# Putting the words of float64 weights together in two PSUM banks instead of in SBUF

## The chip, the cores and the metric

One core of one Trainium2 chip runs the whole program. The metric is the device time of one execution in microseconds (us); of several executions the median counts. Engines are named as the profile names them: PE (TensorE), DVE (VectorE), ACT (ScalarE), POOL (GpSimd) and SP (SyncE, which here issues the DMAs).

## The reference

Three stages follow each other: local and global attention, a dense layer pair with SiLU, and a soft mixture of experts.

```python
scores = scale * q @ k.T + bias          # 4 x 8 heads, 768 positions, 64 wide, banded
x = softmax(scores) @ v                  # 3072 tokens x 512
h = x @ w_in                             # 512 x 2048
x2 = (h * (1.0 / (1.0 + np.exp(-h)))) @ w_out   # 2048 x 512
logits = x2 @ phi                        # 32 slots
# softmax over tokens gathers x2 into slots, experts w1, w2 work on the slots,
# softmax over slots spreads the result over the tokens again
```

`w_in` and `w_out` arrive as float64, all other large inputs as float32. The kernel has to turn the float64 words into numbers that TensorE can multiply.

## The kernel before, in words

Every float32 number goes through TensorE as two float16 parts, a high one and a low one, and a product takes three matmuls. A part pair is made by the helpers `hi` (lines 191 to 195: one scaled copy on ACT, POOL or DVE) and `lo` (lines 199 and 201: value minus high part, on POOL or DVE).

The 3072 tokens are 24 tiles of 128, worked in 8 chunks of 3 tiles. Attention of a tile is a list of items: `split` (makes the parts of q, k and v), `s_step` (scores into the banks `bS`: matmuls of line 293, then line 298 on DVE and the exponential of line 299 on ACT), and `pv_step` (matmuls of line 336 into `bPV`, scaled by line 346). The first tiles run alone; after that the attention items of the next chunk are dealt out between the matmul steps of the present one. A chunk has 16 steps `l1_step` (lines 460 to 462, then tanh in line 464, line 466 and the parts), and then `l2_part` (lines 480 to 482). The order on each engine is not the order of the Python code: a scheduler with a cost model arranges the instructions at build time.

PSUM has eight banks of 128 x 512 float32: `bS` two, `bPV` one, `bW` four in rotation for the steps of both layers, and `bM` one for small sums.

The weights come in 16 pieces of 1 MB (eight of `w_in`, eight of `w_out`); `w_ahead` has SP load the next one as soon as its place in SBUF is free, and `conv(p)` turns piece p into float16 parts. A piece holds 1024 float64 numbers in each partition. What `conv` does to a piece, by line:

- 421 (DVE) makes a 16-bit check value from each high word, and 423 (PE, twice) sums it over the partitions into `bM`;
- 426 (POOL, pieces 2, 3, 4 and 10) or 428 (ACT, the other twelve) writes the top three bits of the low word's mantissa as a 16-bit number over the low half of the low word, in SBUF;
- 429 (DVE) writes the sign over the upper half, and 430 (DVE) xors the shifted high word in: the low word now is a float32 number;
- 440 (ACT) makes the high part;
- 448 (DVE, 11 pieces) makes the low part, or 443 (ACT) and 446 (POOL) do for pieces 0, 3, 6, 9 and 10.

Piece 0 is turned early in the attention of the first tiles, pieces 1 to 7 between the first layer's steps of chunk 0, and pieces 8 to 15 between the second layer's steps of chunk 0. From chunk 1 on there are no weights left to turn.

Of the kernel before, what the change touches and what calls it, by code (L numbers as in the profile page):

```python
# [45 lines left out]
def p2(e):  # L46
    return float(2.0 ** e)
# [39 lines left out]
L3E = 'AAPPPAAAAAPAAAAA'  # L87
LOE = 'PVVPVVPVVPPVVVVV'
# [12 lines left out]
def fast_kernel(tc, keepp, q_l, k_l, v_l, q_f, k_f, n_global, n_local, w_in, w_out, phi, w1, w2, shapes, pick_c, out):  # L101
# [8 lines left out]
    with ExitStack() as ctx:  # L110
# [8 lines left out]
        bank = [psp.tile([128, 512], F32, name=f"bank{i}") for i in range(8)]  # L119
        bS, bPV, bW, bM = bank[0:2], bank[2], bank[3:7], bank[7]  # L120
        turn = [0]
# [6 lines left out]
        one16 = ar.new([2], BF16)  # L128
# [285 lines left out]
        def conv(p):  # L414
# [6 lines left out]
            V.tensor_scalar(out=odd16.bitcast(U16), in0=u16[:, :, 3], scalar1=0x7000, scalar2=0x3000, op0=ALU.bitwise_and, op1=ALU.bitwise_xor)  # L421
            for j in range(2):
                mm(bM[0:1], one16[:, 0:1], odd16[:, 512 * j:512 * j + 512], start=(p + j == 0), stop=(p + j == 16))

            if L3E[p] == "P":
                G.tensor_scalar(out=u16[:, :, 0], in0=by[:, :, 3], scalar1=1.0 / 32, scalar2=-0.484375, op0=ALU.mult, op1=ALU.add)
            else:
                A.activation(out=u16[:, :, 0], in_=by[:, :, 3], func=AF.Copy, scale=1.0 / 32, bias=-0.484375)
            V.tensor_scalar(out=u16[:, :, 1], in0=u16[:, :, 3], scalar1=0x8000, scalar2=None, op0=ALU.bitwise_and)  # L429
            V.scalar_tensor_tensor(out=low, in0=high, scalar=3, in1=low, op0=ALU.logical_shift_left, op1=ALU.bitwise_xor)  # L430
            lowf = ar.view(place[p], [1024, 2], F32)[:, :, 0]
            if p < 8:
                dst = [wih[:, z, :, 256 * p:256 * p + 256] for z in range(2)]
                src = lowf.rearrange("p (k f) -> p k f", k=4)
# [49 lines left out]
        def l2_end(c, m):  # L484
            op = bW[(turn[0] + m) % 4]
# [219 lines left out]
        odd16 = ar.view(ext0 + 16384, [1024], BF16)  # L705
# [12 lines left out]
        G.memset(one16, 1.0)  # L718
# [38 lines left out]
        for c in range(NCH):  # L757
# [34 lines left out]
            if c == 0:  # L792
# [8 lines left out]
                V.memset(odd, 0.0)  # L801
                V.tensor_reduce(out=odd[0:1], in_=bM[0:1], axis=AX.X, op=ALU.max)
# [30 lines left out]
            if c < NCH - 1:  # L833
                turn[0] += n
# [390 lines left out]
```

## Time and profile before

| what | value |
| --- | --- |
| time, median of 3 runs | 766.43 us (765.55 to 767.75) |
| profiled execution, own time | 765.0 us |
| its span, first to last instruction | 763.2 us |
| mean granted TensorE clock | 0.964 |
| PE busy | 683.0 us, 89% |
| DVE busy | 489.0 us, 64% |
| ACT busy | 336.6 us, 44% |
| POOL busy | 324.7 us, 43% |

The shares are means over stages that have different limits, so they say little by themselves. The profiled execution lies 1.8 us over its span, and 1.4 us under the median.

### The profile page before, as it was taken

The page shows a single profiled execution, that of the slowest core. Times are in us where ns is not written, and L with a number is a line of the kernel's source. Part 1 is how long each engine was busy: PE and PEld are TensorE (multiplying, and loading weights), DVE is VectorE, ACT ScalarE, POOL GpSimd, SP SyncE. Part 2 cuts the span into 40 slices and gives each one's busy share as a digit, 9 for nine tenths or more (in the row PEclk, how much of TensorE's full clock was granted, in tenths as well). Part 3 has the DMA queues.
Part 4 walks back from the last instruction along what each step waited for, and adds up shares of the span by engine and source line. Part 5 has one row for each costly group of instructions (what it writes and reads, how often), then busy time and mean ns, then how long its engine had stood idle before and what let it go on. Part 6 is the DMA issues. An engine that isn't in the chain of part 4 may idle for free.

```text
span 763.2 us, 14337 instructions
## 1 busy us (share of the span) xinstructions
PE 683.0 (89%) x5559; PEld 395.0 (52%) x5559; DVE 489.0 (64%) x1108; ACT 336.6 (44%) x855; POOL 324.7 (43%) x267
## 2 busy tenths in 40 slices
PE   2477757598999999999999999999999999998995
PEld 1244423244655565556556654665466546665375
DVE  6999999997775487548735873597266306505232
ACT  7756786553552255245423542454156305303122
POOL 4689684733455356415633673337324320101000
PEclk9978969799999999999999999999999999999997
DMA  6787645565456355733563567354532694295987
GB/s 237 194 249 205 218 87 152 191 181 120 75 125 139 83 113 137 174 75 77 132 138 74 107 137 167 56 111 109 86 43 43 150 320 178 97 357 214 391 330 223
DMA packets 162747, 120.22 MB, mean 158 GB/s; under 512 B 137456, under 2 KB 147184, under 8 KB 156656
## 3 DMA queue, kind: packets, MB, share of 16 engines
q1 hardware_dynamic: 162672, 119.23, 58.4%
q8 instruction: 45, 0.74, 0.4%
q14 instruction: 30, 0.25, 0.1%
HBM read 79.10 MB, written 6.29 MB: 112 GB/s over the span
## 4 chain that ended last, share of the span: by engine, by line
PE 67%; DVE 16%; issue 5%; POOL 4%; DMA 4%; ACT 3%; SPq 0%; ACTq 0%; DVEq 0%; POOLq 0%
PE bank L480 8%; PE bank L481 8%; PE bank L482 8%; PE bank L460 8%; PE bank L462 8%; PE bank L461 8%; PE bank L293 4%; PE bank L336 3%; DVE arena L201 2%; DMA arena<-arena 2%; DVE arena L199 2%; POOL arena L193 2%; PE bank L864 2%; DVE arena L429 2%; PE bank L902 2%
## 5 line engine op out<-in xcount | busy, mean ns | idle before, releaser
L193 POOL TENSOR_SCALAR arena<-arena 128x1024 f16<-128x1024 f32 (+5 forms) x146 | 144.4, 1002 | 237.0 <-ACT arena L299 102.5
L460 PE MATMUL bank<-rows,arena 128*128 128x384 f16 x512 | 168.4, 330 | 6.2 <-ACT arena L191 4.0
L462 PE MATMUL bank<-rows,arena 128*128 128x384 f16 x512 | 168.3, 329 | 0.8 <-DVE arena L448 0.8
L461 PE MATMUL bank<-rows,arena 128*128 128x384 f16 x512 | 168.3, 329 | 0.0
L191 ACT ACTIVATE arena<-bank 128x384 f16<-128x384 f32 (+2 forms) x165 | 81.8, 505 | 177.0 <-DVE bank L466 98.7
L199 POOL TENSOR_TENSOR arena<-arena 128x1024 f16<-128x1024 f32 (+2 forms) x69 | 131.0, 1900 | 41.3 <-ACT arena L191 37.3
L299 ACT ACTIVATE arena<-arena 128x256 f32<-128x256 f32 (+1 forms) x192 | 92.2, 482 | 98.2 <-DVE arena L298 95.3
L481 PE MATMUL bank<-arena 128*128 128x512 f16 x336 | 128.9, 384 | 2.7 <-POOL arena L446 1.9
L480 PE MATMUL bank<-arena 128*128 128x512 f16 x336 | 129.1, 384 | 1.5 <-DVE arena L201 1.5
L482 PE MATMUL bank<-arena 128*128 128x512 f16 x336 | 128.7, 383 | 0.0
L201 DVE SCALAR_TENSOR_TENSOR arena<-bank,arena 128x384 f16<-128x384 f32 (+2 forms) x142 | 81.3, 572 | 32.7 <-ACT arena L191 32.0
L293 PE MATMUL bank<-arena 128*128 128x256 f16 (+3 forms) x432 | 63.4, 288 | 41.5 <-DVE arena L298 23.9
L298 DVE CUSTOM_DVE_ANT_0 arena<-bank,arena 128x256 f32<-128x256 f32 (+1 forms) x192 | 70.5, 395 | 44.2 <-PE bank L293 42.8
L466 DVE SCALAR_TENSOR_TENSOR bank<-arena,bank 128x384 f32<-128x384 f32 x128 | 71.2, 557 | 31.0 <-ACT arena L464 29.8
L199 DVE TENSOR_TENSOR arena<-arena 128x1024 f16<-128x1024 f32 (+2 forms) x50 | 74.7, 1496 | 12.6 <-POOL arena L193 12.2
L464 ACT ACTIVATE arena<-bank 128x384 f32<-128x384 f32 x128 | 61.9, 484 | 21.1 <-PE bank L462 20.8
L293 PEld LDWEIGHTS <-arena 128*128 128x128 f16 (+1 forms) x432 | 36.3, 101 | 66.5 <-issue 38.1
L462 PEld LDWEIGHTS <-arena 128*128 128x128 f16 x512 | 50.4, 99 | 35.4 <-issue 1.6
L461 PEld LDWEIGHTS <-arena 128*128 128x128 f16 x512 | 50.4, 98 | 34.5 <-issue 7.2
L460 PEld LDWEIGHTS <-arena 128*128 128x128 f16 x512 | 50.5, 99 | 31.4 <-issue 2.9
L482 PEld LDWEIGHTS <-arena 128*128 128x128 f16 x336 | 33.1, 99 | 43.9 <-issue 5.3
L480 PEld LDWEIGHTS <-arena 128*128 128x128 f16 x336 | 33.2, 99 | 38.1 <-issue 4.8
(174 smaller groups left out, 808.8 us busy)
## 6 DMA issues: line engine op xcount, KB each, us to landing
arena<-in_w_dram SPq DMA_DIRECT2D x31, 1024.0 KB, 7.4
arena<-in_q_l_dram SPq DMA_DIRECT2D x18, 512.0 KB, 3.7
arena<-in_k_l_dram SPq DMA_DIRECT2D x18, 512.0 KB, 4.0
arena<-in_w_in_dram SPq DMA_DIRECT2D x8, 1024.0 KB, 5.7
arena<-in_w_out_dram SPq DMA_DIRECT2D x8, 1024.0 KB, 4.9
arena<-in_v_l_dram SPq DMA_DIRECT2D x24, 256.0 KB, 3.0
out_dram<-arena SPq DMA_DIRECT2D x4, 768.0 KB, 7.6
out_dram<-arena SPq DMA_DIRECT2D x8, 384.0 KB, 5.0
```

Source lines behind the costliest of these rows:

```text
L191: A.activation(out=out, in_=in_, func=AF.Copy, scale=p2(e))
L193: G.tensor_scalar(out=out, in0=in_, scalar1=p2(e), scalar2=0.0, op0=ALU.mult, op1=ALU.add)
L199: (V if eng == "V" else G).tensor_tensor(out=out, in0=in_, in1=h, op=ALU.subtract)
L201: V.scalar_tensor_tensor(out=out, in0=in_, scalar=p2(e), in1=h, op0=ALU.mult, op1=ALU.subtract)
L293: mm(sp[i][:, :w] if t == 0 else sp[i].rearrange("p (s c) -> p s c", s=2), qd[r, 4 * y + h], kv, start=(j == 0), stop=(j == len(terms) - 1))
L299: A.activation(out=pw, in_=pw, func=AF.Exp, scale=-1.0, bias=nmx[:, T, h:h + 1], accum_out=psum_[T % 2][:, h:h + 1])
L460: mm(hp, wh, x[:, 0, k], start=(k == 0), stop=False)
L461: mm(hp, wh, x[:, 1, k], start=False, stop=False)
L462: mm(hp, wl, x[:, 0, k], start=False, stop=(k == 3))
L480: mm(op, gh, woh[:, f, 0], start=(f == 0), stop=False)
L481: mm(op, gh, woh[:, f, 1], start=False, stop=False)
L482: mm(op, gl, woh[:, f, 0], start=False, stop=(f == 15))
```

## The change

`bank6` and `bank7` become one tile `words` (`bC`). ACT writes the three bits of all 16 pieces there as 32-bit integers, DVE adds the sign and the high word there, and both parts are read from there: the high one by ACT, the low one by DVE. POOL has no part in `conv` any more. The place of a piece in SBUF is given up as soon as the word is complete. The check is a bitwise or that DVE keeps over all pieces, without matmuls; one mask and one maximum follow at the end. While words are in the two banks, chunk 0 has three banks of `bW` for its steps instead of four.

```diff
-        bank = [psp.tile([128, 512], F32, name=f"bank{i}") for i in range(8)]
+        bank = [psp.tile([128, 512], F32, name=f"bank{i}") for i in range(6)]
+
+        bC = psp.tile([128, 1024], F32, name="words")
+        bank += [bC[:, 0:512], bC[:, 512:1024]]
...
-                tb = bW[flips[0] % 4]
+                tb = bW[flips[0] % 3]
...
-            V.tensor_scalar(out=odd16.bitcast(U16), in0=u16[:, :, 3], scalar1=0x7000, scalar2=0x3000, op0=ALU.bitwise_and, op1=ALU.bitwise_xor)
-            for j in range(2):
-                mm(bM[0:1], one16[:, 0:1], odd16[:, 512 * j:512 * j + 512], start=(p + j == 0), stop=(p + j == 16))
-
-            if L3E[p] == "P":
-                G.tensor_scalar(out=u16[:, :, 0], in0=by[:, :, 3], scalar1=1.0 / 32, scalar2=-0.484375, op0=ALU.mult, op1=ALU.add)
-            else:
-                A.activation(out=u16[:, :, 0], in_=by[:, :, 3], func=AF.Copy, scale=1.0 / 32, bias=-0.484375)
-            V.tensor_scalar(out=u16[:, :, 1], in0=u16[:, :, 3], scalar1=0x8000, scalar2=None, op0=ALU.bitwise_and)
-            V.scalar_tensor_tensor(out=low, in0=high, scalar=3, in1=low, op0=ALU.logical_shift_left, op1=ALU.bitwise_xor)
-            lowf = ar.view(place[p], [1024, 2], F32)[:, :, 0]
+            V.scalar_tensor_tensor(out=odd16, in0=u16[:, :, 3], scalar=0x3000, in1=odd16, op0=ALU.bitwise_xor, op1=ALU.bitwise_or)
+
+            word = bC.bitcast(I32)
+            A.activation(out=word, in_=by[:, :, 3], func=AF.Copy, scale=1.0 / 32, bias=-0.484375)
+            V.scalar_tensor_tensor(out=word, in0=high, scalar=-(2 ** 31), in1=word, op0=ALU.bitwise_and, op1=ALU.bitwise_xor)
+            V.scalar_tensor_tensor(out=word, in0=high, scalar=3, in1=word, op0=ALU.logical_shift_left, op1=ALU.bitwise_xor)
+            holder[place[p]] = None
+            w_ahead()
...
             A.activation(out=dst[0], in_=src, func=AF.Copy, scale=-p2(e - 128))
-            if LOE[p] != "V":
-                if LOE[p] == "P":
-                    A.activation(out=src, in_=src, func=AF.Copy, scale=-p2(e - 128))
-                else:
-                    G.tensor_scalar(out=src, in0=src, scalar1=-p2(e - 128), scalar2=0.0, op0=ALU.mult, op1=ALU.add)
-                G.tensor_tensor(out=dst[1], in0=src, in1=dst[0], op=ALU.subtract)
-            else:
-                V.scalar_tensor_tensor(out=dst[1], in0=src, scalar=-p2(e - 128), in1=dst[0], op0=ALU.mult, op1=ALU.subtract)
-            holder[place[p]] = None
-            w_ahead()
+            V.scalar_tensor_tensor(out=dst[1], in0=src, scalar=-p2(e - 128), in1=dst[0], op0=ALU.mult, op1=ALU.subtract)
...
-            hp = bW[turn[0] % 4][:, :n]
-            turn[0] += 1
+            hp = bW[f % 3 if c == 0 else turn[0] % 4][:, :n]
+            if c:
+                turn[0] += 1
...
-                V.memset(odd, 0.0)
-                V.tensor_reduce(out=odd[0:1], in_=bM[0:1], axis=AX.X, op=ALU.max)
+                V.tensor_scalar(out=odd16, in0=odd16, scalar1=0x7000, scalar2=None, op0=ALU.bitwise_and)
+                V.tensor_reduce(out=odd, in_=odd16, axis=AX.X, op=ALU.max)
```

The scheduler's order moves with it. In the changed file the lines of `conv` are 421 (check), 424 (bits, ACT), 425 and 426 (sign and high word, DVE), 437 (high part, ACT) and 438 (low part, DVE); helpers above line 400 keep theirs.

On DVE, among the pieces of `w_out` in chunk 0, these rows stood before; they are the front of two pieces (421, 429, 430) with attention between them:

```order
L421 TENSOR_SCALAR arena<-arena 128x1024
L429 TENSOR_SCALAR arena<-arena 128x1024
L199 TENSOR_TENSOR arena<-arena 128x8x128
L430 SCALAR_TENSOR_TENSOR arena<-arena 128x1024
L346 TENSOR_TENSOR arena<-bank_72,arena 128x512
L421 TENSOR_SCALAR arena<-arena 128x1024
L429 TENSOR_SCALAR arena<-arena 128x1024
L201 SCALAR_TENSOR_TENSOR arena<-arena 128x8x64
L430 SCALAR_TENSOR_TENSOR arena<-arena 128x1024
```

At the same stage DVE now has these rows, the low part of one piece (438) and then the word and the low part of the next:

```order
L421 SCALAR_TENSOR_TENSOR arena<-arena 128x1024
L438 SCALAR_TENSOR_TENSOR arena<-words,arena 128x2x512
L199 TENSOR_TENSOR arena<-arena 64x1024
L199 TENSOR_TENSOR arena<-arena 128x8x128
L425 SCALAR_TENSOR_TENSOR words<-arena,words 128x1024
L201 SCALAR_TENSOR_TENSOR arena<-arena 128x8x64
L426 SCALAR_TENSOR_TENSOR words<-arena,words 128x1024
L421 SCALAR_TENSOR_TENSOR arena<-arena 128x1024
L438 SCALAR_TENSOR_TENSOR arena<-words,arena 128x2x512
```

Before, two pieces could be between 421 and 448 at once; now a piece's 438 always stands before the next piece's 425, since both use `words`.

On ACT, at the end of the conversions, the bits of a piece (424) stand right behind the high part of the piece ahead (437), with exponentials of the attention (299) between:

```order
L437 ACTIVATE arena<-words 128x2x512
L299 ACTIVATE arena<-arena 128x256
L424 ACTIVATE words<-arena 128x1024
L299 ACTIVATE arena<-arena 128x256 x3
L437 ACTIVATE arena<-words 128x2x512
L424 ACTIVATE words<-arena 128x1024
L299 ACTIVATE arena<-arena 128x256 x2
L437 ACTIVATE arena<-words 128x2x512
```

Each 424 now waits for the 438 of the piece ahead on DVE, and each 437 for a 426, so ACT and DVE take turns four times for a piece.

On POOL, in the attention of the first tiles, these rows stood before (321 is a small copy that holds a load back until its place is free):

```order
L446 TENSOR_TENSOR arena<-arena 128x4x256
L321 TENSOR_SCALAR arena<-arena 128x1
L426 TENSOR_SCALAR arena<-arena 128x1024
L321 TENSOR_SCALAR arena<-arena 128x1
L193 TENSOR_SCALAR arena<-arena 128x1024
L199 TENSOR_TENSOR arena<-arena 128x1024
L193 TENSOR_SCALAR arena<-arena 128x2x4x8
L193 TENSOR_SCALAR arena<-arena 128x512
```

Now 446 and 426 are gone from there, and the copies and differences of the attention follow each other:

```order
L321 TENSOR_SCALAR arena<-arena 128x1 x2
L193 TENSOR_SCALAR arena<-arena 128x1024
L193 TENSOR_SCALAR arena<-arena 128x2x4x8
L199 TENSOR_TENSOR arena<-arena 128x1024
L321 TENSOR_SCALAR arena<-arena 128x1
L193 TENSOR_SCALAR arena<-arena 8x1024
L199 TENSOR_TENSOR arena<-arena 128x512
```

On PE the 32 rows of line 423 are gone. Counted over the order up to the first matmul of the last `l2_part` group of chunk 0 (the one that needs piece 15), 25 more matmuls of line 293 and 24 more of line 336 stand ahead of it than before; on DVE, up to the low part of piece 15, ten more of line 298 and one more each of 344, 345 and 346.

## Rows read from the trace of the kernel before

**Rows 1.** The page's busy tenths in 40 slices of 19.1 us.

```profile
PE   2477757598999999999999999999999999998995
DVE  6999999997775487548735873597266306505232
```

**Rows 2.** By stage: PE, PEld, DVE, ACT, POOL busy us (count); granted clock; DMA; GB/s.

```profile
0.00:40.00 40.00, 16.34 (x121) 8.63 (x123) 31.84 (x84) 27.48 (x70) 22.08 (x33) 1.00 0.74 225
40.00:176.50 136.50, 99.03 (x670) 48.99 (x667) 133.06 (x179) 86.31 (x151) 92.45 (x58) 0.86 0.64 179
176.50:763.20 586.70, 567.64 (x4773) 337.36 (x4771) 324.15 (x846) 222.80 (x634) 210.15 (x178) 0.99 0.57 148
```

**Rows 3.** The chain that ended last, around piece 15: start, us, what.

```profile
157.39 2.01 POOL arena L199
...
160.74 5.33 DMA arena<-in_w_out_dram
...
174.76 0.62 DVE arena L421
...
176.10 0.54 PE bank L480
```

**Rows 4.** Groups by line and form, 0 to 176.5 us: the conversion's instructions.

```profile
L430 DVE SCALAR_TENSOR_TENSOR arena<-arena 128x1024 int32<-128x1024 int32 x16 | 28.5, 1789 | 0.0
L429 DVE TENSOR_SCALAR arena<-arena 128x1024 uint16<-128x1024 uint16 x16 | 26.4, 1678 | 0.0
L448 DVE SCALAR_TENSOR_TENSOR arena<-arena 128x1024 f16<-128x1024 f32 x11 | 19.2, 1744 | 0.0
L421 DVE TENSOR_SCALAR arena<-arena 128x1024 uint16<-128x1024 uint16 x16 | 16.0, 1000 | 0.0
...
L428 ACT ACTIVATE arena<-arena 128x1024 uint16<-128x1024 uint8 x12 | 30.0, 2499 | 0.4 <-DMA arena<-in_w_out_dram 0.4
...
L440 ACT ACTIVATE arena<-arena 128x1024 f16<-128x1024 f32 x16 | 18.4, 1148 | 28.1 <-DVE arena L430 26.5 <-DVE arena L448 1.6
...
L446 POOL TENSOR_TENSOR arena<-arena 128x1024 f16<-128x1024 f32 x5 | 12.8, 2550 | 5.2 <-ACT arena L443 5.2
L426 POOL TENSOR_SCALAR arena<-arena 128x1024 uint16<-128x1024 uint8 x4 | 11.7, 2925 | 0.3
...
L423 PE MATMUL bank<-arena 128*1 128x512 bf16 x32 | 10.8, 423 | 3.6 <-DVE arena L421 3.2
```

**Rows 5.** Single lines, 0 to 260 us: duration ns min/median/max, first and last start.

```profile
L430 DVE SCALAR_TENSOR_TENSOR arena<-arena x16: 1170/1770/4234, 23.4 to 170.4; 128x1024 int32<-128x1024 int32 x16
...
L466 DVE SCALAR_TENSOR_TENSOR bank<-arena,bank x33: 547/551/564, 68.7 to 259.7; 128x384 f32<-128x384 f32 x33
...
L448 DVE SCALAR_TENSOR_TENSOR arena<-arena x11: 1215/1626/2767, 50.1 to 175.3; 128x1024 f16<-128x1024 f32 x11
```

**Rows 6.** DVE and POOL in order of time, 139 to 145 us: start, duration.

```profile
139.96 4.23 DVE L430 SCALAR_TENSOR_TENSOR arena<-arena 128x1024 int32<-128x1024 int32 x1
...
141.02 2.10 POOL L446 TENSOR_TENSOR arena<-arena 128x1024 f16<-128x1024 f32 x1
```

**Rows 7.** Groups by line and form, 0 to 176.5 us: attention's instructions.

```profile
L298 DVE CUSTOM_DVE_ANT_0 arena<-bank,arena 128x256 f32<-128x256 f32 x40 | 15.8, 416 | 3.1 <-PE bank L293 1.9 <-POOL arena L193 1.1
L199 DVE TENSOR_TENSOR arena<-arena 128x1024 f16<-128x1024 f32 x8 | 14.4, 1797 | 0.7 <-POOL arena L193 0.7
L201 DVE SCALAR_TENSOR_TENSOR arena<-arena 128x512 f16<-128x512 f32 x9 | 10.4, 1152 | 0.0
...
L298 DVE DVE_READ_ACCUMULATOR2_ANT arena<- 128x1 f32 x54 | 4.3, 80 | 0.0
...
L299 ACT ACTIVATE arena<-arena 128x256 f32<-128x256 f32 x40 | 20.0, 504 | 11.4 <-DVE arena L298 9.4 <-POOL arena L193 2.0
```

**Rows 8.** The chain that ended last, chunk 1: start, us, what.

```profile
187.97 0.44 PE bank L293 x4
...
209.91 0.70 PE bank L336 x24
```

More of the change, by code (lines that the diff above doesn't have):

```diff
@@ L86 @@
 PLE = 'PVPPPV'
-L3E = 'AAPPPAAAAAPAAAAA'
-LOE = 'PVVPVVPVVPPVVVVV'
 BE = 'A'
@@ L127, in fast_kernel @@
         ones16 = ar.new([128], F16)
-        one16 = ar.new([2], BF16)
         csum = ar.new([NTILE], F32)
@@ L419, in conv @@
             u16 = ar.view(place[p], [2048], I32).bitcast(U16).rearrange("p (n e) -> p n e", e=4)
[L421 to L431 removed]
+            V.scalar_tensor_tensor(out=odd16, in0=u16[:, :, 3], scalar=0x3000, in1=odd16, op0=ALU.bitwise_xor, op1=ALU.bitwise_or)
[5 more added lines that the diff above has]
+            w_ahead()
             if p < 8:
                 dst = [wih[:, z, :, 256 * p:256 * p + 256] for z in range(2)]
[L434 removed]
+                src = bC.rearrange("p (k f) -> p k f", k=4)
                 e = E_WI
@@ L437, in conv @@
                 dst = [woh[:, 2 * (p - 8):2 * (p - 8) + 2, z] for z in range(2)]
-                src = lowf.rearrange("p (k f) -> p k f", k=2)
+                src = bC.rearrange("p (k f) -> p k f", k=2)
                 e = E_WO
             A.activation(out=dst[0], in_=src, func=AF.Copy, scale=-p2(e - 128))
-            if LOE[p] != "V":
-                if LOE[p] == "P":
-                    A.activation(out=src, in_=src, func=AF.Copy, scale=-p2(e - 128))
-                else:
-                    G.tensor_scalar(out=src, in0=src, scalar1=-p2(e - 128), scalar2=0.0, op0=ALU.mult, op1=ALU.add)
-                G.tensor_tensor(out=dst[1], in0=src, in1=dst[0], op=ALU.subtract)
-            else:
-                V.scalar_tensor_tensor(out=dst[1], in0=src, scalar=-p2(e - 128), in1=dst[0], op0=ALU.mult, op1=ALU.subtract)
-            holder[place[p]] = None
-            w_ahead()
+            V.scalar_tensor_tensor(out=dst[1], in0=src, scalar=-p2(e - 128), in1=dst[0], op0=ALU.mult, op1=ALU.subtract)
         def l1_step(c, f):
             n = CHUNKS[c] * 128
-            hp = bW[turn[0] % 4][:, :n]
-            turn[0] += 1
+            hp = bW[f % 3 if c == 0 else turn[0] % 4][:, :n]
+            if c:
+                turn[0] += 1
             x, g = xt[c], g_of[CHUNKS[c]]
@@ L476, in l2_part @@
             g = g_of[CHUNKS[c]]
-            op = bW[(turn[0] + m) % 4]
+            op = bW[(m + 1) % 3 if c == 0 else (turn[0] + m) % 4]
             for f in fs:
@@ L484, in l2_end @@
         def l2_end(c, m):
-            op = bW[(turn[0] + m) % 4]
+            op = bW[(m + 1) % 3 if c == 0 else (turn[0] + m) % 4]
             T = first[c] + m
@@ L704, in fast_kernel @@
         glb = ar.view(tb + 3840, [128], F32)
-        odd16 = ar.view(ext0 + 16384, [1024], BF16)
+        odd16 = ar.view(ext0 + 16384, [1024], BF16).bitcast(U16)
         for i, src in enumerate((n_global, n_local)):
@@ L717, in fast_kernel @@
         nc.sync.dma_start(out=ph, in_=phi)
-        G.memset(one16, 1.0)
+        G.memset(ar.view(ext0 + 16384, [512], F32), 0.0)
         hi("P", ident16, ident, 0)
@@ L833, in fast_kernel @@
             if c < NCH - 1:
-                turn[0] += n
+                turn[0] += n if c else 3
             while st["d"] < len(todo):
```

## Prediction

> **What bounds the kernel now.** I read the page's strips first. PE is full from the tenth slice on, DVE is full in the first nine and not afterwards [rows 1]. So the program has two parts with different limits, and the question is where they meet. The view by stage, cut where the last weight piece gets its low part (176.5 us), puts numbers on it: from 40 to 176.5 us DVE is busy 133.06 of 136.5 us and PE 99.03; from there to the end PE is busy 567.64 of 586.70 us at a granted clock of 0.99 [rows 2]. Up to the cut DVE is busy 31.84 + 133.06 = 164.9 us and idle 11.6. The chain that ended last is no pure DVE chain there: near the cut it runs through a POOL difference, a transpose's issue, the load of piece 15 (5.33 us, landed at 166.1) and then through DVE to the last matmuls of chunk 0 [rows 3]. Still, with 97% busy, work taken from DVE ahead of the cut is what can move the cut.
>
> So I forecast two things: when DVE finishes piece 15 (now 176.5 us), and how much PE work is left then (567.64 us, with 19.06 us of idle time, which I leave).
>
> **The change, part by part.** *DVE, removed.* The four instructions of the conversion cost 28.5 + 26.4 + 19.2 + 16.0 = 90.1 us ahead of the cut [rows 4]. Much of this is not their own work: line 430 takes 1.17 us at best and 4.23 at worst, line 448 1.22 to 2.77 [rows 5]. The 4.23 us one lies across POOL instructions, among them line 446, 2.10 us long [rows 6]. Line 466, with one input in PSUM and one in SBUF, takes 547 to 564 ns in all of its 33 runs, beside a POOL that is busy for two thirds of that time [rows 2, 5]. So two inputs in SBUF are slowed by POOL here, and one of each is not.
>
> *DVE, added.* Three instructions for each piece (sign, high word, low part) have one input in PSUM and one in SBUF. From line 298's 416 ns at 256 columns and line 466's 551 at 384 [rows 5, 7] a column costs 1.05 ns, so 1024 columns cost 0.551 + 640 x 0.00105 = 1.22 us: 48 x 1.22 = 58.6 us. The fourth, the or of the check, has two inputs in SBUF. The trace has none in 16 bits; the nearest row is line 448, 1.22 us undisturbed and 1.74 in the mean [rows 4, 5]. I take 1.55, since POOL will be less busy: 24.8 us; bounds 1.22 and 1.86 (19.5 and 29.8 us), the upper one a little over the mean because this instruction has no undisturbed neighbour of its own. Together 83.4, so DVE saves 6.7 us (bounds 12.0 and 1.7).
>
> [...]
>
> *DVE, moved ahead.* The scheduler puts ten more score instructions before piece 15's low part, 10 x (0.416 + 0.080) = 5.0 us [rows 7], with some 1.0 us for one more set of 344 to 346. The end of the check, a mask and a maximum over 1024 columns, adds an estimated 2.2 us (one instruction like line 430 at best, one a little cheaper). Sum 8.2 us.
>
> *POOL.* Lines 446 and 426 go, 12.8 + 11.7 = 24.5 us [rows 4] of 22.08 + 92.45 = 114.5 busy before the cut [rows 2], a fifth. The other DVE instructions with two SBUF inputs pay for POOL as well: lines 199 and 201 in [rows 7] cost 1.80 us at 1024 columns and 1.15 at 512, where 1.22 and 0.69 are the undisturbed cost by the slope above: 8 x 0.58 + 9 x 0.46 = 8.8 us, and the smaller groups an estimated 14 more. A fifth to a quarter of 23 us is 5 us. Bounds: 0 (POOL fills the room with the attention that moves ahead) and 10.
>
> *ACT and the turns.* ACT loses 30.0 us of line 428 and the copies of line 443, and gains 16 conversions into PSUM. No row shows ACT writing integers to PSUM: 2.50 us (line 428, 8-bit in, 16-bit out with gaps) is one bound, line 440's 1.15 us (same gaps on the input, 32-bit in) the other [rows 4]. The cost on DVE is the wait it causes. From 438 of one piece to 425 of the next, DVE has 1.3 to 4 us of other work in its order (the two places shown: two instructions of line 199, about 3 us; elsewhere three scores, 1.5 us). If the conversion takes 1.15 us plus about 0.3 for a running exponential (0.504 us [rows 7]) and the hand-over, nearly every gap covers it; if 2.50, ten of the fifteen gaps are too short and DVE waits about 10 us in all. The output with gaps is gone, which I hold for the likelier reason of line 428's 2.50 us, so I take the low end, with 3 us of waits, since the words allow one piece at a time where before two or three overlapped. Bounds 0 and 12.
>
> [...]
>
> *PE.* 32 matmuls of line 423 (10.8 us) go, at a place where PE waits for DVE anyway: nothing. 25 matmuls of line 293 and 24 of line 336 move ahead of the cut and no longer stand in the full stage: 25 x 0.44/4 + 24 x 0.70/24 = 3.5 us less [rows 8]. Three banks instead of four in chunk 0: a step of 12 matmuls there comes every 4 us or slower, and a bank is drained in about four short instructions, so nothing, or up to 2 us if a drain stands behind a conversion in DVE's queue.
>
> *Loads.* A place is free two instructions earlier, some 2 to 4 us. Piece 15's load was on the chain [rows 3], but behind a transpose in SP's queue, so the gain is not sure; I count nothing, and DVE has other work.
>
> **Sum.** The cut moves by -6.7 + 8.2 - 5 + 3 = -0.5 us and 3.5 us less is left behind it: span 763.2 - 4.0 = 759.2, time 761.0 with the 1.8 us around it. The profiled execution lies 1.4 us under the median of 766.43; I give 761.5. All good ends together: -12.0 + 8.2 - 10 + 0 - 3.5 = -17.3; all bad ends: -1.7 + 8.2 + 0 + 12 + 2 - 3.5 = +17.
>
> **Rivals.**
> 1. *The turns become the bound (slower).* ACT's conversion stays at 2.50 us. Then one piece needs 2.50 + 3 x 1.22 + 1.15 + four hand-overs and the scores between, 8 to 9 us, against some 8.3 us that DVE has for one (125 us for fifteen). Waits of 10 to 12 us in place of 3, some on PE behind them: 767 to 774 us. It decides from a conversion of about 2 us on. For it: lines 426 and 428 take 2.9 and 2.5 us on two engines, and both read bytes. Against: DVE reads 16-bit words at the same gaps and needs 1.00 us (line 421) [rows 4]. 0.25.
> 2. *POOL's relief is larger.* Fewer DVE instructions hold POOL up as well, so POOL ends sooner and meets DVE less; relief 10 us, the or at 1.22: 750 to 756 us. For it: the worst DVE times all lie across POOL work [rows 6]. 0.15.
> 3. *No effect.* DVE's saving is eaten by waits for scores and loads in the new order, since near the cut the chain hangs on POOL and a load [rows 3]: 764 to 769 us. 0.15.
> [...]
>
> **How the numbers follow.** The forecast, 757 to 764 us, gets 0.40. What a measurement can tell from no change is 0.3%, 764.1 to 768.7. Faster: nearly all of the forecast (0.38), rival 2 (0.15), a little of 3 and 4 (0.03): 0.56. Same: 0.02 of the forecast, 0.05 of rival 1, 0.14 of 3 and 4: 0.21. Slower: rival 1's rest and the tail of 3: 0.23. Leaving a tenth out on each side, the range is 752 to 772.
>
> **What the profile would show.** Right: lines 425, 426 and 438 at 1.2 us with hardly a spread, line 421 at 1.2 to 2; ACT's 424 near 1.2; the low part of piece 15 at 172 to 179 us, PE full behind it. Wrong: 424 at 2.5, and DVE idle ahead of 425 for ACT, or 438 for ACT, by more than 5 us in all; PE waiting in chunk 0 for a bank; or, the other way, lines 199 and 201 falling to 1.2 and 0.7 us everywhere.

## Result: 777.65 us, slower by 1.5%, and the profile after

Median of 4 runs 777.65 us (775.15 to 779.64), against 765.99 us for the kernel before in the same session: ratio 1.0149 [1.0115, 1.0184]. The forecast was 761.5 us, the range 752 to 772. The profiled execution took 779.17 us with a span of 777.4, so 14.2 us more span than before. Line numbers below are those of the kernel each fence belongs to; 449 to 451 are the changed kernel's matmuls of the first layer.

The page's busy tenths, changed kernel, in slices of 19.4 us; [rows 1] is the same of before.

```profile
PE   2577857767999989999999999999999999998994
DVE  6799787998664488547755883687276216304232
```

DVE is no longer full from the second to the ninth slice. PE stands at 9 from the eleventh slice on in both kernels (194 us, and 191 us before); in the two slices ahead of it PE is now at 6 and 7, where it was at 9 and 8. By stage, cut where piece 15's low part ends (180.2 us, 176.5 before) and at the end of the last first layer; the columns are those of [rows 2].

```profile
0.00:40.00 40.00, 16.84 (x126) 8.99 (x127) 29.85 (x86) 24.95 (x72) 16.00 (x31) 1.00 0.78 226
40.00:180.20 140.20, 103.42 (x691) 53.07 (x691) 125.57 (x208) 77.65 (x170) 64.35 (x59) 0.87 0.67 182
...
180.20:671.20 491.00, 476.63 (x3806) 278.75 (x3803) 297.70 (x747) 202.22 (x573) 192.54 (x153) 1.00 0.49 112
671.20:777.40 106.20, 92.36 (x914) 53.36 (x911) 28.51 (x75) 17.37 (x41) 8.09 (x17) 0.93 0.79 290
```

The last two stages of before, in the same view:

```profile
176.50:662.70 486.20, 478.79 (x3861) 282.81 (x3859) 296.15 (x771) 205.25 (x593) 202.16 (x161) 1.00 0.51 115
662.70:763.20 100.50, 88.85 (x914) 54.55 (x912) 28.00 (x75) 17.55 (x42) 8.00 (x17) 0.93 0.83 306
```

So of the 14.2 us, 3.7 are a later cut. The middle stage is 4.8 us longer although PE is busy 2.2 us less there: its idle time went from 7.4 to 14.4 us. The tail is 5.7 us longer with the same 914 matmuls, which keep PE busy 3.5 us longer. Three quarters of the loss lie behind the conversion, in a part of the program where the diff changes no instruction of PE's.

What PE waited for there, 185 to 775 us (waiter, releaser: us, times, longest):

```profile
PE words L537 <- DVE arena L201: 3.4, 3, 1.7
PE words L493 <- DMA arena<-arena: 2.7, 1, 2.7
PE bank L449 <- DVE arena L201: 2.3, 1, 2.3
PE words L507 <- DVE arena L201: 1.8, 2, 1.7
PE words L605 <- ACT arena L599: 1.4, 1, 1.4
PE words L449 <- DVE arena L544: 1.2, 1, 1.2
```

All but one are matmuls into "words". Some are of a kind that before had too (L537 was L548 there, 3.9 us); L507, and L449 behind L544, are new. The tile `words` is bank 6 (one of the four that the layers turn through) and bank 7 (logits and slot sums) under one name. The timeline of one such wait:

```profile
276.54 0.55 DVE L455 SCALAR_TENSOR_TENSOR words<-arena,words 128x384 f32<-128x384 f32 x1
277.12 0.49 ACT L191 ACTIVATE arena<-words 128x384 f16<-128x384 f32 x1 [0.71 <-DVE words L455]
277.65 0.56 DVE L201 SCALAR_TENSOR_TENSOR arena<-words,arena 128x384 f16<-128x384 f32 x1 [0.56 <-ACT arena L191]
278.26 0.31 PE L507 MATMUL words<-arena 128*96 128x128 f32 x1 [1.67 <-DVE arena L201]
```

A first-layer step is drained from bank 6 by three instructions in turn. Line 507 transposes the logits into bank 7; it starts 0.05 us behind the last read of bank 6, and the layer's next matmuls stand behind it in PE's queue. Before, the same transpose (L518) started between two matmuls of the layer, without a wait:

```profile
270.79 0.33 PE L462 MATMUL bank<-rows,arena 128*128 128x384 f16 x1
...
270.95 0.27 PE L518 MATMUL bank<-arena 128*96 128x128 f32 x1
```

The conversion itself, 0 to 180.5 us, by form [rows 4 are those of before]:

```profile
L421 DVE SCALAR_TENSOR_TENSOR arena<-arena 128x1024 uint16<-128x1024 uint16 x16 | 24.0, 1498 | 1.1 <-DMA arena<-in_w_out_dram 1.1
...
L425 DVE SCALAR_TENSOR_TENSOR words<-arena,words 128x1024 int32<-128x1024 int32 x16 | 19.6, 1223 | 0.4
L426 DVE SCALAR_TENSOR_TENSOR words<-arena,words 128x1024 int32<-128x1024 int32 x16 | 19.6, 1223 | 0.0
L438 DVE SCALAR_TENSOR_TENSOR arena<-words,arena 128x1024 f16<-128x1024 f32 x16 | 19.4, 1215 | 0.0
...
L424 ACT ACTIVATE words<-arena 128x1024 int32<-128x1024 uint8 x16 | 17.6, 1099 | 14.2 <-DVE arena L438 14.1
...
L437 ACT ACTIVATE arena<-words 128x1024 f16<-128x1024 f32 x16 | 16.4, 1026 | 17.2 <-DVE words L426 17.2
```

The prices are near the forecast's. Behind the bar stands the idle time ahead of each group. ScalarE waits 14.1 us for the words to come free (the low part of the piece before, L438); that wait is new. It waits 17.2 us for them to be made (L426), less than the 26.5 us of before [rows 4]. DVE's own instructions on the words hardly wait: 0.4 us ahead of L425, none ahead of L426 and L438. What DVE waits for, 0 to 180.2 us, is something else:

```profile
DVE bank L455 <- ACT arena L453: 6.6, 4, 3.2
DVE arena L298 <- PE bank L293: 5.7, 5, 1.9
...
DVE arena L199 <- POOL arena L193: 2.2, 1, 2.2
DVE arena L346 <- PE bank L336: 1.7, 2, 1.0
DVE arena L421 <- DMA arena<-in_w_out_dram: 1.1, 1, 1.1
```

Line 453 is a tanh of the first layer. In each of these waits over 0.3 us ScalarE was free for it and waited itself for PE's matmuls (L451). Ahead of the longest one PE had stood for a transpose's landing:

```profile
74.91 0.23 PE L336 MATMUL bank<-arena 128*128 128x64 f16 x1 [3.94 <-DMA arena<-arena]
...
80.59 0.49 ACT L453 ACTIVATE arena<-bank 128x384 f32<-128x384 f32 x1 [6.37 <-PE bank L451]
...
81.12 0.56 DVE L455 SCALAR_TENSOR_TENSOR bank<-arena,bank 128x384 f32<-128x384 f32 x1 [3.21 <-ACT arena L453]
```

Ahead of the others PE had stood for a piece's high part (1.8 us at 84.1, 3.2 us at 112.9). In all it waits 18.9 us for the weights' parts from 60 to 187 us (lines 437 and 438), where before it waited 3.5 us for them (lines 446 and 448, 60 to 183 us). The largest three of now:

```profile
PE bank L469 <- ACT arena L437: 6.3, 3, 3.0
PE bank L470 <- DVE arena L438: 6.1, 6, 2.1
PE bank L449 <- ACT arena L437: 5.2, 3, 3.2
```

### The profile page after: what moved, and what is told of

Its sections match the earlier page's. It is cut to its first block, busy times and chain, and to the rows that moved or that the text cites. A ratio compares the mean times of both kernels' runs of the same rounds, so it can differ in the third digit from the quotient of the medians.

```text
span 777.4 us, 14270 instructions
## 1 busy us (share of the span) xinstructions
PE 689.3 (89%) x5527; PEld 394.2 (51%) x5527; DVE 481.6 (62%) x1113; ACT 322.2 (41%) x854; POOL 281.0 (36%) x258
## 4 chain that ended last, share of the span: by engine, by line
PE 63%; DVE 19%; DMA 6%; ACT 5%; issue 3%; POOL 2%; SPq 0%; ACTq 0%; DVEq 0%; POOLq 0%
PE bank L470 6%; PE bank L471 6%; PE bank L469 6%; PE bank L451 6%; PE bank L449 5%; PE bank L450 5%; DVE arena L199 4%; PE bank L293 3%; PE bank L336 3%; DMA arena<-arena 3%; DVE arena L201 2%; DVE bank L455 2%; PE bank L891 2%; PE words L469 2%; PE words L470 2%
## 5 line engine op out<-in xcount | busy, mean ns | idle before, releaser
L193 POOL TENSOR_SCALAR arena<-arena 128x1024 f16<-128x1024 f32 (+5 forms) x146 | 136.7, 947 | 307.0 <-ACT arena L299 117.9
L449 PE MATMUL bank<-rows,arena 128*128 128x384 f16 x400 | 133.0, 333 | 8.3 <-ACT arena L437 5.2
L199 POOL TENSOR_TENSOR arena<-arena 128x1024 f16<-128x1024 f32 (+2 forms) x69 | 122.4, 1775 | 33.4 <-ACT arena L191 28.3
L450 PE MATMUL bank<-rows,arena 128*128 128x384 f16 x400 | 133.2, 333 | 0.0
L451 PE MATMUL bank<-rows,arena 128*128 128x384 f16 x400 | 132.0, 332 | 1.3 <-DVE arena L438 1.3
L191 ACT ACTIVATE arena<-bank 128x384 f16<-128x384 f32 (+2 forms) x132 | 65.3, 507 | 120.0 <-DVE bank L455 61.4
L470 PE MATMUL bank<-arena 128*128 128x512 f16 x256 | 100.0, 390 | 6.1 <-DVE arena L438 6.1
L469 PE MATMUL bank<-arena 128*128 128x512 f16 x256 | 97.1, 390 | 6.3 <-ACT arena L437 6.3
L471 PE MATMUL bank<-arena 128*128 128x512 f16 x256 | 100.1, 391 | 0.0
L293 PE MATMUL bank<-arena 128*128 128x256 f16 (+3 forms) x432 | 65.0, 289 | 25.8 <-DVE arena L298 14.1
L201 DVE SCALAR_TENSOR_TENSOR arena<-bank,arena 128x384 f16<-128x384 f32 (+1 forms) x107 | 61.4, 574 | 23.8 <-ACT arena L191 23.3
L199 DVE TENSOR_TENSOR arena<-arena 128x1024 f16<-128x1024 f32 (+2 forms) x50 | 68.4, 1374 | 11.6 <-POOL arena L193 11.1
L455 DVE SCALAR_TENSOR_TENSOR bank<-arena,bank 128x384 f32<-128x384 f32 x100 | 55.7, 558 | 30.6 <-ACT arena L453 29.4
L449 PEld LDWEIGHTS <-arena 128*128 128x128 f16 x512 | 50.6, 99 | 37.0 <-ACT arena L437 6.0
L451 PEld LDWEIGHTS <-arena 128*128 128x128 f16 x512 | 50.8, 99 | 36.1 <-DVE arena L438 2.5
L450 PEld LDWEIGHTS <-arena 128*128 128x128 f16 x512 | 50.7, 99 | 35.8 <-issue 7.9
L453 ACT ACTIVATE arena<-bank 128x384 f32<-128x384 f32 x100 | 48.6, 487 | 41.8 <-PE bank L451 41.3
L471 PEld LDWEIGHTS <-arena 128*128 128x128 f16 x336 | 33.4, 99 | 48.1 <-issue 11.1
L336 PE MATMUL bank<-arena 128*128 128x64 f16 x1056 | 43.3, 200 | 14.8 <-DMA arena<-arena 14.8
```

The source lines that it names most:

```text
L193: G.tensor_scalar(out=out, in0=in_, scalar1=p2(e), scalar2=0.0, op0=ALU.mult, op1=ALU.add)
L199: (V if eng == "V" else G).tensor_tensor(out=out, in0=in_, in1=h, op=ALU.subtract)
L201: V.scalar_tensor_tensor(out=out, in0=in_, scalar=p2(e), in1=h, op0=ALU.mult, op1=ALU.subtract)
L293: mm(sp[i][:, :w] if t == 0 else sp[i].rearrange("p (s c) -> p s c", s=2), qd[r, 4 * y + h], kv, start=(j == 0), stop=(j == len(terms) - 1))
L449: mm(hp, wh, x[:, 0, k], start=(k == 0), stop=False)
L450: mm(hp, wh, x[:, 1, k], start=False, stop=False)
```

## The experiments

Theory A: the one tile for two banks makes users of the halves wait for each other, behind the conversion. Theory B: the new conversion itself costs time, because the words allow one piece at a time, or by its order. Each kernel was timed in 3 to 5 rounds beside the kernel before (medians 766.78 to 767.16 us). A theory that tells where the time goes can be held against these differences to before, in us: the start of the last first-layer matmul of each chunk in the timeline, and the span. Each row is one execution.

| | chunk 0 | 1 | 2 | 3 | 4 | 6 | 7 | span |
|---|---|---|---|---|---|---|---|---|
| before, at | 121.35 | 220.91 | 296.67 | 370.68 | 446.10 | 593.22 | 662.66 | 763.2 |
| changed kernel | -0.8 | +3.6 | +6.2 | +7.7 | +7.4 | +8.5 | +8.4 | +14.2 |
| e1, before with one tile | +1.3 | +1.3 | +4.2 | +5.7 | +5.4 | +6.5 | +7.6 | +11.8 |
| e3, changed, tile split | -4.4 | +0.7 | +0.4 | +0.4 | +0.6 | +0.6 | +0.9 | +2.0 |
| e10, half of the tile out of the turn | -2.9 | +1.3 | +1.4 | +1.4 | +1.7 | +1.7 | +1.1 | +6.8 |
| e12, eight one-bank tiles | -3.4 | -5.0 | -4.9 | -4.9 | -4.9 | -4.9 | -4.3 | -4.3 |

The first column and the cut scatter. To about 180 us the traces of the changed kernel, e3 and e10 hold the same instructions in the same order on every engine (the first 847 matmuls and the first 302 instructions of DVE in the changed kernel and e3), yet their low part of piece 15 ends at 180.2, 177.4 and 177.7 us. So some 2.5 of the 3.7 us by which the changed kernel's cut came later are a difference between executions. From chunk 2 to chunk 6 the steps from column to column repeat: in e2, e3 and e12, whose banks are tiles of their own there, they are under 0.4 us.

**e1, the kernel before with nothing but one tile for banks 6 and 7.**

```diff
-        bank = [psp.tile([128, 512], F32, name=f"bank{i}") for i in range(8)]
+        bank = [psp.tile([128, 512], F32, name=f"bank{i}") for i in range(6)]
+        bC = psp.tile([128, 1024], F32, name="words")
+        bank += [bC[:, 0:512], bC[:, 512:1024]]
```

> The kernel before with one edit: banks 6 and 7 are the two halves of one tile, as in the change; the conversion is the old one. Theory A (the two halves are kept apart badly afterwards: users of the fourth step bank and of the small-sums bank wait for each other, which costs the 10 us that the change loses behind chunk 0): 6 to 10 us slower than before, with waits ahead of the matmuls into the halves. Theory B (the loss comes from the turns of ACT and DVE on one word buffer): within 2 us of before. Since the scheduler orders anew, an order alone may move it by some us either way.

778.22 us, 1.0162 [1.0136, 1.0189]: a loss as large as the changed kernel's, with the old conversion, and a little over the 6 to 10 us expected. Four of its waits of PE, 185 to 775 us, are those of the changed kernel to a tenth:

```profile
PE words L550 <- DVE arena L203: 3.4, 3, 1.7
PE words L520 <- DVE arena L203: 1.8, 2, 1.7
...
PE words L618 <- ACT arena L612: 1.4, 1, 1.4
PE words L462 <- DVE arena L557: 1.2, 1, 1.2
```

Steps of the table fall at the same places: +3.0 in chunk 2 (2.6 in the changed kernel), +1.5 in chunk 3 (1.5), +0.7 in chunk 6 (0.7) and +4.2 in the tail (5.8). Of the changed kernel's 2.6 us in chunk 2, 2.3 are more idle time of PE, most of it the wait of L507 shown above. The two differ in chunk 7 (+1.1, -0.1), and the changed kernel's +4.4 in chunk 1 is no part of it: e3 (+5.1) and e10 (+4.2) have it too.

**e3, the changed kernel with the words tile in a pool of its own**, closed behind chunk 0; banks 6 and 7 are then two tiles.

```diff
...
+        bC = wordp.tile([128, 1024], F32, name="words")
+        bank += [None, None]
...
+                wordx.close()
+                latep = ctx.enter_context(tc.tile_pool(name="latep", bufs=1, space=PSUM))
+                bank[6] = bW[3] = latep.tile([128, 512], F32, name="bank6")
+                bank[7] = bM = latep.tile([128, 512], F32, name="bank7")
```

> The changed kernel with one edit: the words' tile is given up behind chunk 0 and banks 6 and 7 are two tiles of their own from there. Theory A: 6 to 10 us faster than the change, 768 to 772 us. Theory B: as the change, 775 to 780 us.

767.60 us, 1.0017 [1.0000, 1.0033]. The loss is gone, from both sides: one tile put in costs 11.8 us of span, taken out it gives 12.2. In the medians it is 11.4 us, and about 10 between the ratios 1.0149 and 1.0017. For theory B 0.8 us are left in the medians (2.0 in the spans), hardly more than the measurement can tell. PE's waits after 185 us:

```profile
PE bank L539 <- DVE arena L203: 4.1, 4, 1.5
PE bank L451 <- DVE arena L203: 2.6, 1, 2.6
PE bank L495 <- DMA arena<-arena: 2.5, 2, 2.0
```

The first is before's own (3.9 us there). The transposes' waits for drains (L507 above) are gone. One rival stays: behind 187 us the tile also gave the scheduler another order. Behind 190 us some 70% of PE's matmuls stand in the same order in the changed kernel and in e3, 98% in e3 and e10. In chunk 2 the step is waiting; how the rest of the loss divides into waiting and order is not separated.

**e10, the changed kernel with its one tile, but the layers turn through banks 3 to 5** in chunks 1 to 7 (the last chunk's second layer keeps four).

```diff
-            hp = bW[f % 3 if c == 0 else turn[0] % 4][:, :n]
+            hp = bW[f % 3 if c == 0 else turn[0] % 3][:, :n]
...
-            op = bW[(m + 1) % 3 if c == 0 else (turn[0] + m) % 4]
+            op = bW[(m + 1) % 3 if c == 0 else (turn[0] + m) % 3]
```

> The changed kernel with its one words tile, but behind chunk 0 the two layers turn through banks 3 to 5 alone, in chunks 1 to 7's first layer and chunks 1 to 6's second, so that the half that is bank 6 stays out of the turn there, and only the last chunk's end uses both halves side by side. If the time goes because users of the two halves wait for each other (theory A), the steps of +2.9 us in chunk 2, +1.4 in chunk 3 and +0.9 in chunks 4 and 6 go and the tail's 5.8 stay: 769 to 773 us, with a turn of three banks adding at most 2. If it is the new conversion or the order of the program: no change, 776 to 780 us.

773.00 us, 1.0092 [1.0060, 1.0123]. The steps in chunks 2 to 7 are gone and the tail's 5.7 us stay (106.2 us from the start of the last first-layer matmul to the end, 106.3 in the changed kernel, 100.5 before). Three banks instead of four cost next to nothing in the steady part.

**e2, the kernel before with three banks in chunk 0**, as the change has it.

```diff
...
-            hp = bW[turn[0] % 4][:, :n]
+            hp = bW[f % 3 if c == 0 else turn[0] % 4][:, :n]
...
```

> The kernel before with one edit: chunk 0 and the early transposes use three of the four step banks, as in the change. Theory C (three banks make PE wait in chunk 0, and the chunk's last sums leave the bank that chunk 1 wants next): 3 to 6 us slower, with PE waiting ahead of line 460 in chunk 0 and at the start of chunk 1. Theories A and B: within 2 us of before.

767.61 us, 1.0012 [0.9996, 1.0029]: no difference that the measurement can tell. That part was rightly costed at nothing to 2 us.

**e4, the kernel before with the check as an or**, without the 32 matmuls of line 423.

```diff
-            V.tensor_scalar(out=odd16.bitcast(U16), in0=u16[:, :, 3], scalar1=0x7000, scalar2=0x3000, op0=ALU.bitwise_and, op1=ALU.bitwise_xor)
-            for j in range(2):
-                mm(bM[0:1], one16[:, 0:1], odd16[:, 512 * j:512 * j + 512], start=(p + j == 0), stop=(p + j == 16))
+            V.scalar_tensor_tensor(out=odd16, in0=u16[:, :, 3], scalar=0x3000, in1=odd16, op0=ALU.bitwise_xor, op1=ALU.bitwise_or)
...
```

> The kernel before with one edit: the check is the bitwise or on DVE, as in the change, and its 32 matmuls are gone. DVE then has 16 instructions of 1.5 us in place of 16 of 1.0 us, 8 us more in a stage where DVE was 97% busy, so if DVE's sum sets that stage the time rises by 6 to 9 us; if waits set it (theory B), by 0 to 3 us. Theory A says nothing on it.

777.32 us, 1.0135 [1.0116, 1.0155], 10.5 us and so more than either expectation. By groups, 0 to 185 us, the or costs 28.4 us there, where line 421 of before costs 16.0 [rows 4]:

```profile
L420 DVE SCALAR_TENSOR_TENSOR arena<-arena 128x1024 uint16<-128x1024 uint16 x16 | 28.4, 1776 | 0.0
```

Chunk 1's first layer starts 3.3 us later, and there PE waits once 3.9 us for the logits' transposes. So beside the old conversion the or is no cheap check. How much of the 10.5 us is the or and how much the other order that the scheduler made is not separated.

**e5, e3 with the or left out of all pieces** (the check sees zeros).

```diff
-            V.scalar_tensor_tensor(out=odd16, in0=u16[:, :, 3], scalar=0x3000, in1=odd16, op0=ALU.bitwise_xor, op1=ALU.bitwise_or)
```

> The split version (words tile freed behind chunk 0, 767.6 us), with the check's or left out of all sixteen pieces (what the check looks at stays zero). It takes 16 instructions, 23.6 us, off VectorE ahead of the cut. If VectorE's sum of work sets the cut (theory S, the one of my prediction), the cut comes 18 to 22 us sooner and the time is 747 to 752 us. If the turns of the one words tile, with the loads and the scores between, set the pace (theory T), VectorE only idles more: the cut moves by less than 8 us and the time is 760 to 767.

760.82 us, 0.9915 [0.9893, 0.9937], 6.8 us less than e3, in the range of theory T. But neither theory's mechanism is seen. VectorE's 23.6 us did not go out of its sum, since the scheduler filled the room with attention (81 scores by 179.3 us; e3 has 65 by its cut). In the same window, e5 first and e3 behind it (columns of [rows 2]):

```profile
0.00:179.30 179.30, 121.46 (x936) 66.81 (x937) 160.72 (x323) 110.29 (x272) 100.36 (x108) 0.92 0.80 223
0.00:179.30 179.30, 121.11 (x841) 63.47 (x842) 157.14 (x297) 104.26 (x246) 82.74 (x91) 0.90 0.70 193
```

VectorE is busy 3.6 us more than in e3, and chunk 1's first layer starts 1.3 us later. So e5 does not decide between theory S (VectorE's sum sets the cut), on which my prediction stood, and theory T. What the time went into is attention moved ahead: PE has 95 more matmuls behind it at 179.3 us, and e5 is 6.7 us ahead of e3 at the end of chunk 2's first layer (5.7 in the span).

**e7, e3 with the odd pieces' words in SBUF**, so that two pieces in a row never share the tile.

```diff
+            if p % 2:
+                A.activation(out=u16[:, :, 0], in_=by[:, :, 3], func=AF.Copy, scale=1.0 / 32, bias=-0.484375)
+                V.tensor_scalar(out=u16[:, :, 1], in0=u16[:, :, 3], scalar1=0x8000, scalar2=None, op0=ALU.bitwise_and)
+                V.scalar_tensor_tensor(out=low, in0=high, scalar=3, in1=low, op0=ALU.logical_shift_left, op1=ALU.bitwise_xor)
...
```

> The split version, but the odd pieces keep their words in SBUF (ScalarE for the bits, VectorE for sign, high word and low part, all in place), so that two pieces in a row never share the words tile. The count of VectorE instructions stays; eight times three of them have two SBUF inputs or a 16-bit form again, 1.0 to 1.8 us instead of 1.22, so -2 to +10 us on VectorE's sum. Theory T (turns): ScalarE's and VectorE's waits for the words tile go down by more than 10 us and the cut comes 3 to 6 us sooner: 762 to 765 us. Theory S (sum): no gain, 767 to 773 us.

766.25 us, 0.9990 [0.9977, 1.0002]: between the two expectations, 1.4 us under e3. Chunk 1 starts at 173.1 us, 8.5 sooner than in the kernel before; then PE waits 3.9 us at 181.3 for the logits' transposes, and at the end of chunk 1's first layer 2.7 us of lead are left. Most of the lead does not arrive. DVE is busy 150.8 us and idle 19.0 to its cut at 169.8 us, in e3 155.3 and 22.1 to 177.4, with 54 scores ahead of it and not 65. So less work ahead of the cut goes with the earlier cut as well as shorter turns do.

**e8, e3 with two words tiles of one bank**, each piece in two halves of 512 columns.

```diff
...
+            for q in range(2):
+                word = bC[q].bitcast(I32)
+                cut = slice(512 * q, 512 * q + 512)
+                A.activation(out=word, in_=by[:, cut, 3], func=AF.Copy, scale=1.0 / 32, bias=-0.484375)
+                V.scalar_tensor_tensor(out=word, in0=high[:, cut], scalar=-(2 ** 31), in1=word, op0=ALU.bitwise_and, op1=ALU.bitwise_xor)
...
```

> The split version with two words tiles of one bank each, every piece in two halves of 512 columns: twice the instructions, each with about 0.14 us of fixed cost, so 48 x 0.14 = 7 us more on VectorE and 32 x 0.2 = 6 us on ScalarE, but the second half's turn lies beside the first's. Theory T: the turns get shorter by about half, the waits go, and the time stays or falls a little (763 to 768 us) in spite of the larger sum. Theory S: 772 to 776 us.

761.87 us, 0.9935 [0.9915, 0.9956], 5.7 us under e3 with twice the instructions. Its groups, 0 to 175 us:

```profile
L430 DVE SCALAR_TENSOR_TENSOR words<-arena,words 128x512 int32<-128x512 int32 x32 | 21.8, 689 | 0.0
L429 DVE SCALAR_TENSOR_TENSOR words<-arena,words 128x512 int32<-128x512 int32 x32 | 21.7, 688 | 0.0
L443 DVE SCALAR_TENSOR_TENSOR arena<-words,arena 128x512 f16<-128x512 f32 x32 | 21.5, 685 | 0.4 <-ACT arena L442 0.3
```

Three groups cost 65.0 us instead of the changed kernel's 58.6, as expected (ScalarE's two 39.2 instead of 34.0), and the time falls all the same, even under the 763 to 768 us of theory T. That shorter turns did it is not shown. To the cut, e8 first and e3 behind it:

```profile
0.00:171.70 171.70, 116.50 (x787) 58.83 (x788) 149.34 (x318) 101.27 (x256) 74.45 (x80) 0.92 0.66 189
0.00:177.40 177.40, 119.21 (x832) 62.52 (x833) 155.27 (x293) 102.69 (x241) 80.84 (x89) 0.90 0.71 195
```

VectorE's idle time is the same, 22.4 and 22.1 us; what is less is its other work, with 57 scores ahead of the cut and not 65. PE's waits for the weights' parts, 60 to 187 us, did not get shorter either: 23.8 us in e8, 18.3 in e3. The largest two in e8:

```profile
PE bank L454 <- ACT arena L442: 8.8, 5, 2.4
PE bank L474 <- ACT arena L442: 8.7, 5, 4.6
```

So the cut came sooner in the same measure as VectorE had less work ahead of it. Whether two shorter turns made the scheduler deal out less attention there, or the other order is the gain by itself, is not separated.

**e6 and e9, two tries to keep the lead at chunk 1's start.** e6 is e3 with chunk 0's sums in the banks in the order in which they end; e9 is e8 with chunk 0's logits two steps later, and e11 the kernel before with the same shift, as a control. The first edit below is e6's, the second that of e9 and e11.

```diff
-            op = bW[(m + 1) % 3 if c == 0 else (turn[0] + m) % 4]
+            op = bW[m % 3 if c == 0 else (turn[0] + m) % 4]
...
-            at(2 if c == 0 else CFG["lag_l"], lambda: logits(c, m))
+            at(4 if c == 0 else CFG["lag_l"], lambda: logits(c, m))
```

> The split version, with chunk 0's three sums in banks 0, 1, 2 of the four in the order in which they end, so that chunk 1's second step takes the bank that was drained first and not the one drained last. In the split version PE waits 2.57 us there and 2.02 us a little later for a transpose. If that bank order is what eats the 4.4 us that the split version is ahead at the end of chunk 0's first layer, 763 to 766 us. If PE would only wait for the transposes instead: 767 to 768.

> The version with two words tiles (761.87 us), with chunk 0's logits put two steps of the program later (4 instead of 2). There PE waited 3.69 us at 181.6 us for the first logits' transpose, and its clock fell to half for 3.4 us behind it, some 1.7 us more; 8.3 us of lead at chunk 1's start became 3.1 at the end of its first layer. If that wait is what takes the lead: 756 to 759 us. If something else in chunk 1 takes it (the drains of chunk 0's sums, the attention's scores): 761 to 763.

> The kernel before, with chunk 0's logits two steps later, as a control for the two-words version with that shift. There PE waited no more than about 1 us for the logits of chunk 0, so 0 to 1.5 us less: 765 to 767 us.

e6: 767.79 us, 1.0021 [0.9999, 1.0043], no gain. e9: 762.28 us, 0.9937 [0.9914, 0.9961], no gain over e8. e11: 766.78 us, 0.9995 [0.9978, 1.0012]. In e9 the logits wait for the same transposes, only in one piece:

```profile
181.21 1.23 SPq L487 DMA_TRANSPOSE arena<-arena  x1
...
185.54 0.51 PE L498 MATMUL bank<-arena 128*128 128x32 f16 x12 [4.81 <-DMA arena<-arena]
```

The third transpose is issued at 181.21 us, and the logits wait until 185.5. Moving them two steps moved the wait, not its end.

**e12, the changed kernel with eight one-bank tiles as before, and the words in halves in banks 6 and 7.** The simplest form of e8: no instruction spans two banks.

```diff
-        bC = psp.tile([128, 1024], F32, name="words")
-        bank += [bC[:, 0:512], bC[:, 512:1024]]
+        bank = [psp.tile([128, 512], F32, name=f"bank{i}") for i in range(8)]
+        bC = bank[6:8]
...
```

> The changed kernel with eight tiles of one bank each, as before, and every piece's words in two halves of 512 columns, one in bank 6 and one in bank 7: no instruction spans two banks, and no tile has to be freed behind chunk 0. By both findings so far (users of the halves wait for each other, and one turn of words is too few) it should run like the version with two words tiles of their own: 760 to 763.5 us. If the separate pool, freed behind chunk 0, had a share in that version's gain: 764 to 768.

761.25 us, 0.9929 [0.9911, 0.9947]: faster than before by 0.7%, and no share of the separate pool in e8's gain is seen. Its stages, cut at its own last low part and last first-layer matmul:

```profile
40.00:170.40 130.40, 100.53 (x666) 50.90 (x665) 118.34 (x231) 76.94 (x184) 56.06 (x50) 0.91 0.62 177
170.40:658.40 488.00, 476.53 (x3830) 281.24 (x3828) 296.95 (x769) 205.03 (x591) 202.59 (x161) 0.99 0.53 117
658.40:758.90 100.50, 89.01 (x914) 54.44 (x912) 28.00 (x75) 17.56 (x42) 7.99 (x17) 0.93 0.83 306
```

The tail is before's 100.5 us again, and the cut is 6.1 us earlier than before.

## Why the prediction was wrong

The span came out 18.2 us over the 759.2 of the sum: the cut 4.2 us later than the 176.0 forecast (180.2), PE's busy time behind it 4.9 us more than the 564.1 (568.99), and its idle time 9.1 us more (28.2 against 19.06). In e3, without the shared tile, the three are 177.4, 564.4 and 23.4 us: the tile took both more idle time and longer busy time of PE.

**The step that failed: "19.06 us of idle time, which I leave".** The part of the diff that makes bank 6 and bank 7 one tile was costed for chunk 0 only (three banks instead of four). Its price falls behind the cut, where I took PE's idle time over from the kernel before. e1 shows it alone and e3 the change without it, and they agree on the places: 3.0 us in chunk 2, 1.5 in chunk 3, 4.2 to 4.7 in the tail. The rest of their 12 us is spread differently (3.5 us in chunk 0 between the changed kernel and e3, which is the scatter of one order in two executions; 1.3 in e1, with another order). e10 shows that the steps in the chunks go with the half that is in the layers' turn. None of the rivals had this mechanism either; the range ended 5.7 us under the result. The trace shows that the matmul into one bank did not overlap the drain of the other under the one name: PE waited 1.67 us ahead of 278.26 us for a drain of the other bank. What is shown is that the loss goes with the tile, since e12 uses the same two banks without it and takes 761.25 us; the matmul starts 0.05 us behind the drain's end.

In the tail, bank 6 and bank 7 hold the two halves of a hidden layer, each drained by another engine and then transposed in place. In before the transposes end at 724.3 us, ahead of the next stage's first matmul (725.1 us); in the changed kernel they end at 737.6, 3.8 us behind it (733.8), in among its matmuls. Of the 5.7 us, 3.5 are longer busy time of the same matmuls. I read this from the timeline; no experiment split the tail further.

**The cut: the parts were right, their sum was not.** The conversion's four groups measured 82.6 us (83.4 forecast). Eleven more scores stand ahead of the cut (65 against 54; ten forecast). DVE is busy 155.4 us to the cut, where 164.9 - 6.7 + 8.2 leaves 166.4, so by difference 11 us of relief from POOL and not 5, about the 10 of rival 2; no run shows that relief alone. With POOL busy 80.4 us to the cut, 114.5 before, line 199 at 1024 columns took 1.48 us in the mean, 1.80 before, and line 201 at 512 columns 0.80, 1.15 before [rows 7]; line 199 at 512 columns took 0.97, 0.91 before. But DVE is idle 24.8 us, where 11.6 + 3 were forecast. The step "work taken from DVE ahead of the cut is what can move the cut" is the one that fell: 9.5 us less work than before went with 13.2 us more idle time, and in e3, with the same order and its cut at 177.4 us, 9.6 us less with 10.5 us more.

**The waits.** The 3 us that I took for DVE's waits from the turns were not the term that grew. ScalarE's conversion came out at the low end, 1.10 us, so the condition of rival 1 (2 us or more) was not met, and DVE waited 0.4 us ahead of its three instructions on the words. The 13.2 us are in other waits: 6.6 us for the tanh of line 453, where before had none; 5.7 us for scores (3.3 from PE before); 1.7 us for line 336 (none before), 2.2 for line 193 (0.7) and 1.1 for a load (none). The tanh waited for PE, and PE had waited for the weights' parts or for a transpose. My sum had no term for DVE waiting on the first layer's steps. Whether the turns are behind PE's 18.9 us stays open: e8 and e12, with two shorter turns side by side, are 5.7 and 6.4 us faster than e3 with about 6 us more of VectorE's work on the words, but with fewer scores ahead of the cut, and with VectorE nearly as long idle (22.4, 20.0 and in e3 22.1 us).

My reading of [rows 1] was loose as well: PE's tenth slice is at 8, and DVE's first at 6.

**The check.** The or cost 1.50 us in the mean, 1.55 forecast, one of them 3.14. Without it the kernel is 6.8 us faster (e5), by attention that moved into its place.

**PE and chunk 0's banks.** Between the cut and the tail PE was busy 2.2 us less (3.5 forecast). Three banks cost nothing (e2).

**VectorE's instructions on the words.** The 48 instructions with a PSUM source took 1.215 to 1.223 us in the mean, with hardly a spread (1.207 to 1.230 us); the forecast was 1.22, and line 448 took 1.215 us from SBUF at best [rows 5]. The 4 in the prediction's chances stands for PSUM words that cost more than that, and no run shows such a cost.

What stays open: what sets the landing of chunk 0's transposes near 182 to 185 us. All versions with an earlier cut (e7, e8, e9, e12) give 3 to 6 us of their lead back there.

## What to carry to other kernels

In this kernel a PSUM tile was a unit of waiting. Two banks under one name cost it 10 to 12 us, most of it in stages where the diff changes no instruction of PE's, and whoever gives a bank a second use should list every later user of each half and look for one that the other half's drain would now hold up. When an engine looks 97% busy, ask what it would wait for next, and what the scheduler will put in the room, before counting removed work as time: here 9.5 us less work went with 13.2 us more waiting, and 23.6 us taken out were filled with other work. Before a gain is put down to shorter turns, look whether the waits got shorter: in e8 they did not.

## What was not expected of the hardware

ScalarE's conversion of bytes to 32-bit integers in PSUM took 1.10 us for 1024 columns, against 2.50 us for bytes to 16-bit words with gaps in SBUF [rows 4], though both read the same bytes; what of this is the output's gaps, its width or its place was not tried. A VectorE instruction with PSUM took 1.223 us for 1024 columns and 0.688 for 512, so by an estimate from these two, 2 x 0.688 - 1.223 = 0.15 us of it does not depend on the columns. The or of 16-bit values took 1.27 to 1.78 us in the mean in four kernels (e8, e12, the changed kernel and e4), most where POOL was busiest ahead of the cut (117.2 us to 185 us in e4, 80.4 to 180.2 in the changed kernel, 74.0 to 170.4 in e12, 74.4 to 171.7 in e8).
